# A planner that keeps VectorE's and GpSimd's work on SBUF apart, a memory part one unit later, and weight preparation in pieces

## The chip, the cores and the metric

The kernel runs on one core of a Trainium2 chip. Its time is the device time of one execution in microseconds, as the median of several. The engines are named as in the profile: PE (TensorE, matmuls), DVE (VectorE), ACT (ScalarE), POOL (GpSimd), and SP, whose queue issues the DMAs.

## The reference

Attention with a linear memory beside it, then two feed-forward layers. B, H, S, D = 4, 8, 576, 64; 2304 tokens, width 512, inner widths 2048 and 1536; all in float32.

```python
scores = q @ k.T / sqrt(D), causal mask -1e9
a = exp(scores - max);  a /= a.sum + 1e-9;  local = a @ v
q_p = phi(q)                                  # where(x > 0, x, exp(x) - 1) + 1
mem_out = (q_p @ M_prev) / (q_p @ z_prev + 1e-6)
attn = g * mem_out + (1 - g) * local          # g = sigmoid(beta), by head
h = attn @ w_in;  h = softplus(h) @ w_out
out = ((h @ w_a) * (h @ w_b)) @ w_2
```

## The kernel before

**Attention.** Sixteen units, each a pair of heads of one batch (`Unit`, L428 to L614). Keys and queries are split into a rounded high part and a remainder (`kh`, `kl`, `qh`, `ql`; `prep_k`, made on POOL and ACT, for the first two units on DVE), and a score product is three matmuls: high x high, high x low, low x high (L470, L486). `score(i)` handles rows 128 i to 128 i + 127 of both heads, `score(4)` the 64 rows that are left. DVE reads a score bank, adds the mask, takes the extremum along the row into `mn` and writes the tile `e` (L474, L487; the page calls the instruction CUSTOM_DVE_ANT_0); ACT takes the exponential and sums it into `sm`. `memory` (L494) multiplies `ph`, the phi of the queries, by M and z (L504), takes the reciprocal of the norm in `nm` (L508, L510) and scales the result into `mo` on DVE (L512). `sums` (L517) makes `ss`, the softmax sums, on POOL and scales `mo` by it, also on POOL (L524); `over` makes `rs`, the reciprocals of `ss` (L528, DVE), and spreads them into `R` (L530, POOL). `turn` transposes the exponentials (L541) and copies them scaled by 1 - g into `aT` on ACT (L547) or DVE (L549). `spread` transposes `R` and adds `mo` into the output bank (L585, L589); `use` and `finish` multiply by v (L577, L601, L607) and write `xx`, scaled by `R` (L597, L608).

The loop (L632 to L668) works on two units at once: iteration n scores unit n (`cur`) and finishes unit n-1 (`prev`). `memory` of `cur` stands between `score(1)` and `score(2)`. PE's instructions keep this order. The scores and the memory part take turns on two pairs of PSUM banks, so `score(2)` follows `memory`'s neighbour, and `memory` needs the bank pair that DVE read for `score(0)`, `score(3)` the one from which DVE read `mo`.

**Feed-forward layers.** Each of the layers multiplies by a seven-product scheme over halves of the matrices (`Seven`, L793 and L941). A left part of `w_in`, `w_a` or `w_b` is made by `left_parts`: `decode` turns 64-bit words into float32 in five operations on `raw` (L688, L689 and L691, L693 on DVE, L690 on ACT), then come four sums `wf` (L705), a rounding on ACT and the remainder `w` (L307, DVE). `right_parts` does the like for the inputs, tiles `x1h`, `x1l` and so on. The first three left parts (`FIRST`) and the parts of the first and second third of the attention's output, X[0] and X[1], are made during the attention; the text below calls all of it preparation. The feed-forward matmuls start at the end of the last unit, since they use the same banks.

**The order of the work.** Nothing is issued directly. `Engine` records every operation with its operands as a `Step`; `weigh` (L149) gives it a time, `order` (L198) runs a list schedule over the five engines (on DVE, ACT, POOL and SP the step with the highest rank among those that are ready, on PE the recorded order, attention ahead of the rest), and `emit` issues the result with a wait for every dependence. Each engine then works in that fixed order. Where DVE and POOL both work on SBUF plays no part in `weigh` or `order`.

Of the kernel before, what the change touches and what calls it, by code (L numbers as in the profile page):

```python
# [35 lines left out]
class Step:  # L36


    __slots__ = ("n", "eng", "call", "kw", "line", "deps", "after", "time", "lag", "size", "rank", "stream", "mode", "left", "ready", "start")

# [12 lines left out]
class Plan:  # L53
# [95 lines left out]
    def weigh(self, s):  # L149
# [4 lines left out]
        inp = lambda ap: hasattr(ap, "tensor") and ap.tensor.name == self.psum  # L154
        s.size, s.mode, n = 0, None, size(o)
        if call == "dma_start":
            run = min(self.run(o), self.run(kw["in_"]))
# [3 lines left out]
        elif s.eng == "PE":  # L161
            s.lag = 205
            if call == "transpose":
                s.time = n / 1.2 + 3
                s.mode = 128, 128
            else:
                plain = kw["rhs"].dtype != F32R
                rows, cols = (64 if x <= 64 else 128 for x in (kw["lhsT"].partition_size(), size(kw["lhsT"])))
                s.time = max(2 * (n / 1.2 + 3) if plain else n / 2.4 + 13.3, cols * 0.42 * (128 // rows))
                s.time /= 16384 / rows / cols  # L170
                s.mode = rows, cols
        elif s.eng == "DVE":
            s.lag = 125
            two = call in ("tensor_tensor", "scalar_tensor_tensor", "tensor_tensor_reduce")
            s.time = n / (0.96 if two or any(inp(v) for v in kw.values()) else 1.92) + 68
            if hasattr(kw.get("scalar1"), "tensor"):
                s.time += 64
        elif s.eng == "ACT":
            s.lag = 50 if "accum_out" in kw else 145
            s.time = n * 0.834 + (50 if inp(kw["in_"]) else 94) + (184 if "accum_out" in kw else 0)  # L180
            if not isinstance(kw.get("scale", 1.0), float) or kw.get("scale") == REBIAS:
                s.time += 90
        else:
            s.lag = 90
            s.time = n * 2.1 + 250 if call == "tensor_tensor" else n * 0.9 + 230

# [11 lines left out]
    def order(self):  # L198
# [17 lines left out]
        for s in steps:  # L216
            if not s.left:
                heapq.heappush(soon[s.eng], (0.0, s.n))
        t, lane, done, mode, landed = 0.0, 0.0, 0, None, []
        while done < len(steps):  # L220
            nxt = float("inf")
            moved = False
            for e in engines:
# [10 lines left out]
                if not now[e]:  # L234
                    if soon[e]:
                        nxt = min(nxt, soon[e][0][0])
                    continue
                s = steps[heapq.heappop(now[e])[1]]
                s.start = t
                end = t + s.time  # L240
                if e == "PE":
                    if s.mode != mode:
                        end += SWITCH
                    mode = s.mode
# [43 lines left out]
def tile_kernel(ctx: ExitStack, tc: tile.TileContext, qt, kt, vt, mp, zp, be, w_in, w_out, w_a, w_b, w_2, out):  # L288
# [137 lines left out]
    class Unit:  # L426
# [67 lines left out]
        def memory(self):  # L494
# [6 lines left out]
            for c0, n in ((0, 3), (3, 2)):  # L501
# [7 lines left out]
                pms.append((c0, n, s))  # L509
            V.reciprocal(out=nm, in_=nm)  # L510
            for c0, n, s in pms:
                V.tensor_tensor(  # L512
# [4 lines left out]
        def sums(self):  # L517
# [4 lines left out]
            self.at = []  # L522
            m4 = self.mo.rearrange("p c (j e) -> p c j e", j=2)
            G.tensor_tensor(out=m4, in0=m4, in1=heads(ss, 5), op=ALU.mult)  # L524

# [92 lines left out]
    def attention():  # L618
# [15 lines left out]
        for n in range(nu + 1):  # L634
# [47 lines left out]

    def decode(src, to):

        raw = take("raw").bitcast(U32).rearrange("p (m c) -> p m c", c=2)
        SP.dma_start(out=raw, in_=src)
        low, high = raw[:, :, 0], raw[:, :, 1]
        V.tensor_scalar(out=low, in0=low, scalar1=29, scalar2=None, op0=ALU.logical_shift_right)  # L688
        V.scalar_tensor_tensor(out=low, in0=high, scalar=0x80000000, in1=low, op0=ALU.bitwise_and, op1=ALU.bitwise_or)  # L689
        A.activation(out=f(high), in_=f(high), func=AF.Identity, scale=REBIAS)  # L690
        V.tensor_scalar(out=f(high), in0=f(high), scalar1=MOST, scalar2=-MOST, op0=ALU.min, op1=ALU.max)  # L691
        four = lambda t: t.rearrange("p (b n) -> p b n", b=4)
        V.scalar_tensor_tensor(  # L693
            out=to.bitcast(U32), in0=four(high), scalar=3, in1=four(low), op0=ALU.logical_shift_left, op1=ALU.bitwise_or
        )

    def left_parts(src, at):
# [3 lines left out]
        decode(src, d[:, 0:4])  # L701
# [9 lines left out]
    def right_parts(src, at):  # L711

# [11 lines left out]
        def parts(n, b):  # L724
            rnd(A, x[n][0], b)
            sub(V, x[n][1], b, f(x[n][0]))

# [114 lines left out]

    def left1(u):
        W1[u] = left_parts(w_in[u], at_w[u % 3])

# [12 lines left out]
    for u in FIRST:  # L858
        left1(u)

# [279 lines left out]
```

## Time and profile before

| | |
|---|---|
| median of 3 runs | 1006.91 us (1006.03 to 1007.2) |
| the profiled execution | 1008.35 us, span 1006.6 us |
| PE, DVE, ACT, POOL busy | 962.2, 817.5, 561.9, 115.4 us |
| instructions of PE, DVE, ACT, POOL | 6220, 1312, 1036, 132 |
| PE on the chain that ended last | 76%, DVE 17% |
| POOL's last busy slice | the tenth of 40 slices: the attention |

Busy time counts the instructions that execute, not waits between them; a DVE instruction that is held up by POOL counts as busy while it is held. The granted clock (PEclk) is the share of TensorE's full speed. A unit of attention is taken here as the time from the end of one group of L607 matmuls, the last on PE for a unit, to the end of the next: 33.53, 49.11, 63.45, 78.81, 95.81, 113.53, 125.99, 138.84, 151.57, 164.41, 181.02, 193.47, 205.92, 219.07, 231.66 and 241.91 us.

### The profile page before, as it was taken

The numbers are of one execution on the slowest core, as the hardware profiler recorded it, in microseconds if no ns is written. First come the engines' busy times: TensorE is split into PE (matmuls) and PEld (weight loads), VectorE is DVE, ScalarE is ACT, GpSimd is POOL, SyncE is SP. The second block draws the span as 40 slices with busy tenths as digits, with TensorE's granted clock in tenths as the row PEclk, the third lists the DMA queues.
The fourth block names the chain that finished last, engine by engine and source line by source line (L and its number), as shares of the span: only waits on it lengthen the run. The fifth ranks groups of instructions, "written<-read, shape, count | busy, mean of one in ns | idle before, by whom it ended". The sixth has DMA issues, their size and how long they took to land.

```text
span 1006.6 us, 16653 instructions
## 1 busy us (share of the span) xinstructions
PE 962.2 (96%) x6220; PEld 915.0 (91%) x6220; DVE 817.5 (81%) x1312; ACT 561.9 (56%) x1036; POOL 115.4 (11%) x132
## 2 busy tenths in 40 slices
PE   5987998999999999999999989799999999999998
PEld 4766777778999999999999989799999999999998
DVE  5999899887779853799958997789887665899683
ACT  6776887866666656654545654344443424554453
POOL 4554454441000000000000000000000000000000
PEclk9999899999999999999999999899999999999999
DMA  7342443314888857928273134354663225725611
GB/s 217 106 125 81 115 129 117 105 37 136 267 287 282 290 176 243 330 83 262 84 222 123 67 99 146 114 196 154 221 223 121 104 103 156 253 82 186 205 63 48
DMA packets 76129, 159.96 MB, mean 159 GB/s; under 512 B 11280, under 2 KB 57360, under 8 KB 70928
## 3 DMA queue, kind: packets, MB, share of 16 engines
q1 hardware_dynamic: 75760, 158.57, 47.8%
q8 instruction: 49, 0.80, 0.3%
q10 hardware_dynamic: 288, 0.33, 0.1%
q14 instruction: 32, 0.26, 0.1%
HBM read 104.35 MB, written 54.53 MB: 158 GB/s over the span
## 4 chain that ended last, share of the span: by engine, by line
PE 76%; DVE 17%; issue 2%; DMA 2%; POOL 1%; ACT 1%; DVEq 0%; ACTq 0%; POOLq 0%
PE bank L793 42%; PE bank L941 20%; PE bank L470 3%; PE bank L541 3%; PE bank L577 3%; DVE t L307 2%; PE bank L486 1%; PE bank L589 1%; DVE wf L705 1%; PE bank L504 1%; DVE raw L307 1%; DVE gx2l L307 1%; DVE eFalse L474 1%; DVE gx1l L307 1%; DVE w L307 1%
## 5 line engine op out<-in xcount | busy, mean ns | idle before, releaser
L310 DVE TENSOR_TENSOR s<-bank,s 128x384 f32<-128x384 f32 x216 | 117.2, 553 | 74.5 <-PE bank L793 70.1
L771 ACT ACTIVATE s<-bank 128x384 f32<-128x384 f32 x72 | 34.9, 487 | 88.4 <-PE bank L793 38.3
L793 PE MATMUL bank<-x1h,w 128*128 128x384 f32 x240 | 72.1, 340 | 7.0 <-ACT w L300 3.6
L307 DVE TENSOR_TENSOR t<-t,t 128x1536 f32<-128x1536 f32 (+1 forms) x48 | 74.5, 1555 | 0.8
L793 PE MATMUL bank<-x5h,w 128*128 128x384 f32 x240 | 71.5, 338 | 3.2 <-DVE s L310 3.2
L793 PE MATMUL bank<-x6h,w 128*128 128x384 f32 x240 | 71.2, 337 | 0.0
L793 PE MATMUL bank<-x2h,w 128*128 128x384 f32 x240 | 71.1, 337 | 0.0
L793 PE MATMUL bank<-x4h,w 128*128 128x384 f32 x240 | 71.1, 337 | 0.0
L793 PE MATMUL bank<-x3h,w 128*128 128x384 f32 x240 | 70.5, 334 | 0.0
L793 PE MATMUL bank<-x7h,w 128*128 128x384 f32 x240 | 70.5, 334 | 0.0
L768 ACT ACTIVATE s<-bank 128x384 f32<-128x384 f32 x72 | 34.6, 485 | 42.3 <-PE bank L793 28.3
L690 ACT ACTIVATE raw<-raw 128x1024 f32<-128x1024 f32 x34 | 39.1, 1150 | 29.4 <-DVE raw L689 26.6
L828 ACT ACTIVATE s<-s 128x384 f32<-128x384 f32 x72 | 36.9, 523 | 29.2 <-DVE s L310 29.1
L300 ACT ACTIVATE gx1h<-t 128x768 fp32r<-128x768 f32 x37 | 31.3, 847 | 37.9 <-PE bank L941 32.7
L793 PEld LDWEIGHTS bank<-x1h,w 128*128 128x128 f32 x240 | 44.6, 190 | 8.4 <-DVE w L307 4.3
L300 ACT ACTIVATE gx2h<-t 128x768 fp32r<-128x768 f32 x37 | 31.3, 846 | 34.8 <-PE bank L941 29.7
L300 ACT ACTIVATE gx0h<-t 128x768 fp32r<-128x768 f32 x37 | 31.3, 846 | 31.9 <-PE bank L941 23.6
L478 ACT ACTIVATE eTrue<-eTrue,mn 128x384 f32<-128x384 f32 (+1 forms) x64 | 42.2, 661 | 11.8 <-DVE mn L474 11.8
L793 PEld LDWEIGHTS bank<-x5h,w 128*128 128x128 f32 x240 | 44.7, 190 | 3.6 <-DVE s L310 3.5
L774 ACT ACTIVATE s<-bank 128x384 f32<-128x384 f32 x72 | 35.2, 489 | 22.0 <-PE bank L793 16.3
L470 PE MATMUL bank<-kh,qh 64*128 64x128 f32 (+3 forms) x128 | 31.8, 425 | 15.2 <-DVE kh L302 9.7
L300 ACT ACTIVATE w<-wf 128x1792 fp32r<-128x1792 f32 x20 | 34.1, 1704 | 21.3 <-DVE wf L705 21.0
(329 smaller groups left out, 3132.8 us busy)
## 6 DMA issues: line engine op xcount, KB each, us to landing
gs<-s SPq DMA_DIRECT2D x96, 192.0 KB, 4.1
t<-gs SPq DMA_DIRECT2D x24, 768.0 KB, 4.9
us<-s SPq DMA_DIRECT2D x72, 192.0 KB, 3.1
t<-us SPq DMA_DIRECT2D x12, 768.0 KB, 4.7
raw<-w_in SPq DMA_DIRECT2D x8, 1024.0 KB, 6.1
raw<-w_out SPq DMA_DIRECT2D x8, 1024.0 KB, 7.0
raw<-w_a SPq DMA_DIRECT2D x6, 1024.0 KB, 5.6
raw<-w_b SPq DMA_DIRECT2D x6, 1024.0 KB, 5.7
```

Of the source, the lines that this page charges most:

```text
L300: A.activation(out=o, in_=i, func=AF.Copy)
L307: eng.tensor_tensor(out=o, in0=a, in1=b, op=ALU.subtract)
L310: eng.tensor_tensor(out=o, in0=a, in1=b, op=ALU.add)
L470: PE.matmul(out=s[:, j, :L], lhsT=a[r, qc], rhs=b[r, 0:L], start=t == 0, stop=t == 2)
L478: A.activation(out=e, in_=e, func=AF.Exp, scale=-1.0, bias=mn[:, n : n + 1], accum_out=sm[:, n : n + 1])
L690: A.activation(out=f(high), in_=f(high), func=AF.Identity, scale=REBIAS)
L768: A.activation(out=self.s1, in_=bank["b"], func=AF.Copy)
L771: A.activation(out=self.s5, in_=bank["c"], func=AF.Copy)
L774: A.activation(out=self.s2, in_=bank["b"], func=AF.Copy)
L793: PE.matmul(out=o, lhsT=w(n, a, k), rhs=x[n][c][:, k], start=start and k == t == 0, stop=k == 1 and t == 2, skip_group_check=True,)
L828: A.activation(out=s, in_=s if bank is None else bank, func=AF.Softplus)
L941: PE.matmul(out=o, lhsT=self.w[n][a][:, u, 128 * m : 128 * m + 128], rhs=x[c][:, j], start=start and u == t == 0, stop=u == self.nu - 1 an ...
```

## The change

`weigh` marks steps that use SBUF in a way that can meet the other engine's: every POOL step, and a DVE step of more than 64 columns that neither reads nor writes PSUM. While such a step of one engine runs in the plan, `order` starts none of the other: it takes another ready step, or lets the engine stand. A marked POOL step also gets a real dependence on the last marked DVE step before it; a DVE step gets none on POOL. `memory` is called for `prev` instead of `cur`, behind the first two `turn`s, and once more after the last unit; the factor `ss` is multiplied into `nm` (128x10, DVE) in place of POOL's instruction on `mo` (128x640). `decode` of the first three left parts works in two halves, their rounding and remainder in four pieces of two, two, two and one seventh; the parts of X[0] are rounded and subtracted in two halves.

```diff
@@ weigh
+        two = call in ("tensor_tensor", "scalar_tensor_tensor", "tensor_tensor_reduce")
+        s.port = s.eng == "POOL" or s.eng == "DVE" and not any(inp(v) for v in kw.values()) and n > 64
@@ order
-        t, lane, done, mode, landed = 0.0, 0.0, 0, None, []
+        t, lane, done, mode, landed, held = 0.0, 0.0, 0, None, [], {"DVE": 0.0, "POOL": 0.0}
+        port = None
...
-                s = steps[heapq.heappop(now[e])[1]]
+                s = steps[now[e][0][1]]
+                if s.port and held[e] > t:
+                    free_ = [x for x in now[e] if not steps[x[1]].port]
+                    if not free_:
+                        nxt = min(nxt, held[e])
+                        continue
+                    s = steps[min(free_)[1]]
+                now[e].remove(next(x for x in now[e] if x[1] == s.n))
+                heapq.heapify(now[e])
                 s.start = t
                 end = t + s.time
+                if s.port:
+                    held["POOL" if e == "DVE" else "DVE"] = end
+                    if e == "DVE":
+                        port = s.n
+                    elif port is not None:
+                        s.deps.add(port)
@@ Unit.memory, Unit.sums
             V.reciprocal(out=nm, in_=nm)
+            V.tensor_tensor(out=nm, in0=nm, in1=self.ss, op=ALU.mult)
...
-            m4 = self.mo.rearrange("p c (j e) -> p c j e", j=2)
-            G.tensor_tensor(out=m4, in0=m4, in1=heads(ss, 5), op=ALU.mult)
@@ attention
+            if cur:
+                cur.prep_v2()
             if prev:
                 prev.turn(A, [(0, 0)])
                 prev.turn(V, [(1, 0)])
-            if cur:
-                cur.prep_v2()
-                cur.memory()
-            if prev:
+                prev.memory()
                 prev.turn(A, [(0, 1), (0, 3)])
@@ decode
-    def decode(src, to):
+    def decode(src, to, step=4):
...
+        for b in range(0, 4, step):
+            low, high = (four(raw[:, :, i])[:, b : b + step] for i in range(2))
...
@@ left_parts
-        rnd(A, w[:, :, 0], d)
-        sub(V, w[:, :, 1], d, f(w[:, :, 0]))
+        for n in range(0, 7, step):
+            e = min(n + step, 7)
+            rnd(A, w[:, n:e, 0], d[:, n:e])
+            sub(V, w[:, n:e, 1], d[:, n:e], f(w[:, n:e, 0]))
@@ right_parts
-            rnd(A, x[n][0], b)
-            sub(V, x[n][1], b, f(x[n][0]))
+            for k in range(0, 2, step):
+                u = slice(k, k + step)
+                rnd(A, x[n][0][:, u], b[:, u])
+                sub(V, x[n][1][:, u], b[:, u], f(x[n][0][:, u]))
@@ feed-forward, before the first unit
     for u in FIRST:
-        left1(u)
+        left1(u, 2)
+    X[0] = right_parts(xs[0], X_AT[0], 1)
```

The order of DVE's instructions where one unit passes into the next, before, in the unit that ends at 95.81 us: `ph`, preparation (`wf`), `xx` of the unit that ends, then the first score reads (ISA) of the next.

```order
L457 SCALAR_TENSOR_TENSOR ph_77<-ph_77,pos_78 128x640
L705 TENSOR_TENSOR wf<-wf 128x256 x3
L528 RECIPROCAL rs_129<-ss_127 128x10
L705 TENSOR_TENSOR wf<-wf 128x256 x3
L597 TENSOR_TENSOR xx_118<-bank,rb_117 128x512
L608 TENSOR_TENSOR xx_118<-bank,rb_117 128x64
L705 TENSOR_TENSOR wf<-wf 128x256
L474 ISA eFalse_87,mn_122<-bank,mask_56 128x128
```

The same place after, two units later in the program (L473 is L457 of before, L720 L705, L323 L307, L490 L474):

```order
L473 SCALAR_TENSOR_TENSOR ph_76<-ph_76,pos_78 128x640
L323 TENSOR_TENSOR w<-wf,w 128x2x256
L323 TENSOR_TENSOR w<-wf,w 128x256
L720 TENSOR_TENSOR wf<-wf 128x256 x3
L612 TENSOR_TENSOR xx_118<-bank,rb_117 128x512
L543 RECIPROCAL rs_129<-ss_127 128x10
L623 TENSOR_TENSOR xx_118<-bank,rb_117 128x64
L490 ISA eFalse_87,mn_122<-bank,mask_56 128x128
```

The preparation stands between `ph` and `xx`, in pieces; none is left between `xx` and the score reads.

DVE behind the first score reads of a unit, before: the whole remainder `w` of a left part, then the memory part of the current unit.

```order
L307 TENSOR_TENSOR w<-wf,w 128x7x256
L508 TENSOR_SCALAR nm_125<-bank 128x6
L508 TENSOR_SCALAR nm_125<-bank 128x4
L510 RECIPROCAL nm_125<-nm_125 128x10
L512 TENSOR_TENSOR mo_101<-bank,nm_125 128x384
L512 TENSOR_TENSOR mo_101<-bank,nm_125 128x256
```

After, the same place, with the memory part of the unit before:

```order
L323 TENSOR_TENSOR w<-wf,w 128x2x256
L564 TENSOR_SCALAR aT_106<-bank,og_60 128x512
L524 TENSOR_SCALAR nm_125<-bank 128x6
L720 TENSOR_TENSOR wf<-wf 128x256
L524 TENSOR_SCALAR nm_125<-bank 128x4
L526 RECIPROCAL nm_125<-nm_125 128x10
L527 TENSOR_TENSOR nm_125<-nm_125,ss_127 128x10
L529 TENSOR_TENSOR mo_101<-bank,nm_125 128x384
L529 TENSOR_TENSOR mo_101<-bank,nm_125 128x256
```

A remainder of two sevenths and one `wf` stand there, and L527 is the new multiplication.

POOL's order in one unit, before:

```order
L304 TENSOR_SCALAR kh_73<-kr_65 128x576
L307 TENSOR_TENSOR kl_75<-kr_65,kh_73 128x576
L521 TENSOR_SCALAR ss_127<-sm_121 128x9
L521 TENSOR_SCALAR ss_127<-sm_121 128x1
L524 TENSOR_TENSOR mo_101<-mo_101,ss_127 128x640
L530 TENSOR_SCALAR R_104<-rs_129 128x512
L307 TENSOR_TENSOR ql_71<-qr_67,qh_69 128x640
```

And after:

```order
L320 TENSOR_SCALAR kh_72<-kr_64 128x576
L323 TENSOR_TENSOR kl_74<-kr_64,kh_72 128x576
L538 TENSOR_SCALAR ss_126<-sm_120 128x9
L538 TENSOR_SCALAR ss_126<-sm_120 128x1
L323 TENSOR_TENSOR ql_70<-qr_66,qh_68 128x640
L545 TENSOR_SCALAR R_104<-rs_128 128x512
```

`mo` is gone, and `ql` stands ahead of `R`.

## Rows read from the trace of the kernel before

**Rows 1.** The page, busy time by engine.
```profile
PE 962.2 (96%) x6220; PEld 915.0 (91%) x6220; DVE 817.5 (81%) x1312; ACT 561.9 (56%) x1036; POOL 115.4 (11%) x132
```
**Rows 2.** Windows: length, busy time by engine (count), granted clock, DMA share, GB/s.
```profile
33.53:231.66 198.13, 181.67 (x1695) 144.26 (x1696) 180.87 (x476) 149.45 (x392) 95.71 (x96) 0.96 0.32 97
...
241.91:1006.60 764.69, 749.07 (x4273) 746.01 (x4273) 605.72 (x762) 385.31 (x581) 0.00 (x0) 0.99 0.52 173
```
**Rows 3.** Windows, four single units (PE, PEld, DVE, ACT, POOL).
```profile
63.45:78.81 15.36, 12.91 (x124) 9.88 (x123) 15.10 (x36) 10.71 (x28) 9.59 (x9) 1.00 0.28 80
95.81:113.53 17.72, 14.95 (x123) 12.01 (x123) 16.55 (x37) 12.04 (x29) 6.70 (x7) 0.81 0.23 69
164.41:181.02 16.61, 13.67 (x124) 11.33 (x123) 15.27 (x36) 10.42 (x28) 7.08 (x8) 0.90 0.38 122
181.02:193.47 12.45, 12.41 (x123) 9.83 (x123) 9.31 (x31) 9.68 (x27) 6.77 (x9) 1.00 0.26 76
```
**Rows 4.** Waits of PE, 33.53 to 231.66: total us, times, longest.
```profile
PE bank L504 <- DVE mn L474: 10.3, 5, 2.9
PE bank L470 <- DVE mo L512: 5.1, 6, 1.9
```
**Rows 5.** Timeline of PE: start, us, instruction, in brackets the wait before it.
```profile
66.70 1.38 PE L504 MATMUL bank<-mz,ph 128*128 128x130 f32 x10 [1.34 <-DVE mn L474]
...
169.26 2.53 PE L504 MATMUL bank<-mz,ph 128*128 128x130 f32 x10 [2.94 <-DVE mn L474]
```
**Rows 6.** Timeline of all engines, 74 to 80, the SBUF instructions of DVE and POOL.
```profile
74.46 1.40 POOL L307 TENSOR_TENSOR kl<-kr,kh 128x576 fp32r<-128x576 f32 x1
...
75.17 1.37 DVE L457 SCALAR_TENSOR_TENSOR ph<-ph,pos 128x640 f32<-128x640 f32 x1
...
75.94 1.78 POOL L521 TENSOR_SCALAR ss<-sm 128x9 f32<-128x9 f32 x2
...
77.81 1.26 POOL L524 TENSOR_TENSOR mo<-mo,ss 128x640 f32<-128x640 f32 x1
...
77.89 4.34 DVE L705 TENSOR_TENSOR wf<-wf 128x256 f32<-128x256 f32 x4
...
79.04 0.79 POOL L530 TENSOR_SCALAR R<-rs 128x512 f32<-128x512 f32 x1
```
**Rows 7.** Timeline of DVE, 12.5 to 14.1, where POOL does nothing.
```profile
12.53 0.82 DVE L307 TENSOR_TENSOR ql<-qr,qh 128x640 fp32r<-128x640 f32 x1
13.26 0.82 DVE L457 SCALAR_TENSOR_TENSOR ph<-ph,pos 128x640 f32<-128x640 f32 x1
```
**Rows 8.** Lines by form, DVE, from 242 on (no POOL): busy us, mean ns | idle before.
```profile
L705 DVE TENSOR_TENSOR wf<-wf 128x256 f32<-128x256 f32 x68 | 28.8, 423 | 1.6
...
L307 DVE TENSOR_TENSOR raw<-raw,raw 128x768 f32<-128x768 f32 x12 | 11.3, 953 | 0.1
```
**Rows 9.** Lines by form, DVE, 33.53 to 231.66.
```profile
L457 DVE SCALAR_TENSOR_TENSOR ph<-ph,pos 128x640 f32<-128x640 f32 x13 | 16.1, 1236 | 0.0
...
L705 DVE TENSOR_TENSOR wf<-wf 128x256 f32<-128x256 f32 x12 | 10.0, 836 | 0.2
...
L307 DVE TENSOR_TENSOR raw<-raw,raw 128x768 f32<-128x768 f32 x5 | 8.1, 1625 | 0.0
...
L307 DVE TENSOR_TENSOR x2l<-raw,x2h 128x768 fp32r<-128x768 f32 x2 | 2.9, 1442 | 0.0
...
L307 DVE TENSOR_TENSOR x7l<-raw,x7h 128x768 fp32r<-128x768 f32 x1 | 2.0, 1992 | 0.0
```
**Rows 10.** Lines by form, POOL, 33 to 232.
```profile
L524 POOL TENSOR_TENSOR mo<-mo,ss 128x640 f32<-128x640 f32 x15 | 20.2, 1347 | 1.3
L307 POOL TENSOR_TENSOR kl<-kr,kh 128x576 fp32r<-128x576 f32 x12 | 17.0, 1413 | 1.0
...
L304 POOL TENSOR_SCALAR kh<-kr 128x576 fp32r<-128x576 f32 x12 | 8.1, 674 | 76.0 <-PE bank L486 76.0
```
**Rows 11.** Timeline of PE, the first unit's memory part.
```profile
12.65 2.54 PE L504 MATMUL bank<-mz,ph 128*128 128x130 f32 x10 [0.85 <-POOL mz L419]
```

More of the change, by code (lines that the diff above doesn't have):

```diff
@@ L36 @@
 class Step:
-    __slots__ = ("n", "eng", "call", "kw", "line", "deps", "after", "time", "lag", "size", "rank", "stream", "mode", "left", "ready", "start")
+    __slots__ = ("n", "eng", "call", "kw", "line", "deps", "after", "time", "lag", "size", "rank", "stream", "mode", "port", "left", "ready", "start")
 class Engine:
@@ L173, in weigh @@
             s.lag = 125
-            two = call in ("tensor_tensor", "scalar_tensor_tensor", "tensor_tensor_reduce")
             s.time = n / (0.96 if two or any(inp(v) for v in kw.values()) else 1.92) + 68
@@ L184, in weigh @@
             s.lag = 90
-            s.time = n * 2.1 + 250 if call == "tensor_tensor" else n * 0.9 + 230
+            s.time = n * 2.1 + 250 if two else n * 0.9 + 230
     @staticmethod
@@ L681, in tile_kernel, with left_parts @@
     PASSES = ((0, 0), (0, 1), (1, 0))
-    def decode(src, to):
+    def decode(src, to, step=4):
         raw = take("raw").bitcast(U32).rearrange("p (m c) -> p m c", c=2)
         SP.dma_start(out=raw, in_=src)
[L687 to L691, printed above, removed]
-        four = lambda t: t.rearrange("p (b n) -> p b n", b=4)
[L693 to L697, printed above, removed]
+        four = lambda t: t.rearrange("p (b n) -> p b n", b=4)
+        for b in range(0, 4, step):
+            low, high = (four(raw[:, :, i])[:, b : b + step] for i in range(2))
+            V.tensor_scalar(out=low, in0=low, scalar1=29, scalar2=None, op0=ALU.logical_shift_right)
+            V.scalar_tensor_tensor(out=low, in0=high, scalar=0x80000000, in1=low, op0=ALU.bitwise_and, op1=ALU.bitwise_or)
+            A.activation(out=f(high), in_=f(high), func=AF.Identity, scale=REBIAS)
+            V.tensor_scalar(out=f(high), in0=f(high), scalar1=MOST, scalar2=-MOST, op0=ALU.min, op1=ALU.max)
+            V.scalar_tensor_tensor(
+                out=to.bitcast(U32)[:, b : b + step], in0=high, scalar=3, in1=low, op0=ALU.logical_shift_left, op1=ALU.bitwise_or
+            )
+    def left_parts(src, at, step=7):
         w, d = (t.rearrange("p (n h m) -> p n h m", n=7, h=2) for t in twice("w", 3584, at))
         d = d[:, :, 1]
-        decode(src, d[:, 0:4])
+        decode(src, d[:, 0:4], min(step, 4))
         a21, a22, a11, a12 = (d[:, n] for n in range(4))
@@ L705, in left_parts, with right_parts @@
             V.tensor_tensor(out=o, in0=a, in1=b, op=op)
-        rnd(A, w[:, :, 0], d)
-        sub(V, w[:, :, 1], d, f(w[:, :, 0]))
+        for n in range(0, 7, step):
+            e = min(n + step, 7)
+            rnd(A, w[:, n:e, 0], d[:, n:e])
+            sub(V, w[:, n:e, 1], d[:, n:e], f(w[:, n:e, 0]))
         slot = {5: 0, 4: 1, 1: 2, 2: 3, 7: 4, 6: 5, 3: 6}
         return lambda n, h, k: w[:, slot[n], h, 128 * k : 128 * k + 128]
-    def right_parts(src, at):
+    def right_parts(src, at, step=2):
         x = {
@@ L841, in spill_out, with left1 @@
             SP.dma_start(out=wod[:, :, u], in_=t)
-    def left1(u):
-        W1[u] = left_parts(w_in[u], at_w[u % 3])
+    def left1(u, step=7):
+        W1[u] = left_parts(w_in[u], at_w[u % 3], step)
     def made1(i, u, g):
```

## The prediction

> **What bounds the kernel now.** I read the page first, then busy time by stretch, then the attention unit by unit. PE is busy 96% of the span and DVE 81% [rows 1], but these are means over two stages. The span falls into a start of 33.53 us (the first unit), fourteen more units of attention in 198.13 us, a last one of 10.25 us, and 764.69 us in which PE is busy 749 [rows 2]. What the change rewrites lies in the first 242 us; behind that the engines' instructions keep their order almost word for word, so I look for the result in the 198.13 us.
>
> A unit has a floor there. The one from 181.02 takes 12.45 us with PE busy 12.41 at full clock; DVE needs 9.31 and has no weight preparation in it. The unit from 63.45 takes 15.36 with DVE busy 15.10, and the one from 95.81 17.72 with DVE 16.55 and PE at a granted clock of 0.81, in which it is busy 14.95 for the same work [rows 3]. So DVE, loaded with preparation, makes a unit long. The waits say the same: PE waits 10.3 us at L504 for `mn`, that is, until DVE has read the first scores and their bank is free, and 5.1 us at L470 for `mo` [rows 4]. Behind a wait of 2.94 us L504 x10 takes 2.53, behind one of 1.34 it takes 1.38 [rows 5]: a long wait also costs clock. Fourteen units at 12.45 would be 174.3 us, so 23.8 us is all that can be had here.
>
> Part of DVE's load is waiting for POOL where both work on SBUF. At 75.17 `ph` takes 1.37 us, and POOL's `kl` runs until 75.86; at 77.89 four small subtractions `wf` take 4.34 us while POOL runs `mo` and `R` [rows 6] and then `ql`. Alone, `ph` takes 0.82 [rows 7], a `wf` 0.423 and `raw` 128x768 0.953 [rows 8]; the `x` differences have the same 768 columns. In the fourteen units they take 1.236 (x13), 0.836 (x12), 1.625 (x5), and two `x` groups 1.442 (x2) and 1.992 [rows 9]. The excess: 13 x 0.42 = 5.4, 12 x 0.41 = 5.0, 5 x 0.67 = 3.4, 2 x 0.49 + 1.04 = 2.0: 15.8 us of DVE's 180.87 [rows 2]. Smaller groups are left uncounted.
>
> **The change, part by part.** *POOL's `mo` goes.* That is 15 x 1.35 = 20.2 us of POOL in this stretch [rows 10], and the instruction that ran into the preparation. In its place DVE multiplies 128x10, which the trace does not show. From 256 columns at 0.423 and 768 at 0.953 [rows 8] a column costs 1.04 ns and an instruction 0.16 us besides; that is my price, bounds 0.1 and 0.25: 14 x 0.16 = 2.2 us more on DVE.
>
> *Pieces.* DVE gets 21 instructions more for the three weights and 7 for the `x` parts. By the same 0.16, of which I take half since the next one starts before the last has ended (`ph` starts 0.09 before the end of `ql` in [rows 7]): 28 x 0.08 = 2.2 us; bounds 0 and 4.5. ACT gets 19 pieces more; at a full 0.16 and twice that it is at most 6 us beside its 149.45 of 198.13 [rows 2], which PE's work covers.
>
> *The new order.* Before, preparation stands in clumps: none in the unit from 181.02, seven `wf` and a `w` of 1792 columns in others, the `w` ahead of `nm` and `mo`, for which PE waits. After, each unit from the second to the twelfth has three to five pieces behind `ph` and one or two small ones by `nm`. The sum over the fourteen units stays nearly the same: what the slack units lacked is moved into them. This is what shortens the path, since a unit at the floor has 12.45 - 9.31 = 3.1 us of DVE to give.
>
> *The port.* POOL's `kh`, `ql` and most of `R` now stand beside score and copy instructions that read PSUM; the slowed groups of [rows 9] are all SBUF to SBUF. But `kl` is made to wait for `ph`, and right behind `ph` come the pieces. Only POOL gets a wait: in the plan DVE stands idle during `kl`, on the chip it starts its first piece, `kl` follows, and the second piece stands behind `kl`. Price: 1.41 [rows 10] less 0.1 for the start, 1.3 us, in the eleven units with at least two pieces there: 14.3 us. Bounds: 0, if POOL never gets in between, and 11 x 1.41 = 15.5. I take the upper side, since at 77.8 us `mo`, `wf`, `R`, `wf` take turns: four `wf` need 1.7 alone and took 2.6 more, of which `mo` and `R` hold 1.26 and 0.79 [rows 6], and `ql` the rest.
>
> By the Trainium skill (Perfetto Trace Analysis, GPSIMD Engine Instruction) a POOL span in a profile is unreliable, and the spacing of starts is the better measure. From `kl` at 74.46 to `ss` at 75.94 the spacing is 1.48 us against a span of 1.40 [rows 6]; the trace bears it out a little, and by the spacing the eleven units would cost 0.9 us more.
>
> *Waits added.* `kh`, `kl`, `ss`, `ql` and `R` each wait for DVE's last SBUF instruction. Behind them on POOL stands the `ql` of the next unit, needed almost a unit later; POOL waits 76.0 us for PE at `kh` [rows 10], which is its slack, some 5 us a unit: no cost until it is used up. `ss` now comes behind the pieces; DVE's `rs`, which needs it, has `xx` and mostly the score reads in front: nothing, or 0.3 a unit if `ss` is slow. `memory` moves from the current to the previous unit at the same place of PE's stream; its `mo` is due only at the end of that iteration. The weight loads on SP keep their order against each other.
>
> *Start and end.* The first unit loses its L504, 2.54 us behind a wait of 0.85 [rows 11]; but the second unit's `kh`, `kl`, `ql` (0.82 for `ql` [rows 7]) move behind all five score reads, and PE then waits for them, some 2 us; the last unit gains an L504 of about 1.3 [rows 5]. 3.4 - 2.0 - 1.3: nothing, bounds -2 and +2.5.
>
> **The sum.** DVE in the fourteen units: 180.9 - 15.8 + 14.3 + 2.2 + 2.2 = 183.8 us, 13.1 a unit, above PE's 12.45. A DVE-bound unit leaves DVE idle 15.36 - 15.10 = 0.26 [rows 3], 14 x 0.26 = 3.6: 187.4 against 198.1. The last two of the fourteen have no `kl`, and shares of lighter units carry over: about 1 us less. Gain 12. The profiled execution took 1008.35 us, 1.75 around its span; the median of the runs is 1006.91, from which I subtract: 995.
>
> **Rivals.**
> *A: the port wait really goes.* The pieces hide `kl`, or POOL loses each race. For it: behind `ph` PE has some 3 us of products that need DVE for nothing. Against: the turns in [rows 6]. DVE 183.8 - 14.3 = 169.5 is below PE's floor; 174.3 and 0.2 a unit make 177, a gain of 21: 986.
> *B: more collisions than `kl`.* `R` (0.79 at 79.04 [rows 6]) runs into the small pieces by `nm`, and these and the new multiplication hold up `mo`, for which L470 waits already [rows 4]. 11 x 0.5 takes 5.5 of the gain: 1000.5. By the Trainium skill (SBUF — State Buffer, Who interferes with whom) issue order decides which of the two blocks, for the whole instruction; by that rule every POOL instruction that starts first is paid by DVE, which has no wait on POOL here.
> *C: no change.* What the spreading gains is lost again, in POOL's waits or behind 242 us: 1006.
> *D: slower.* The pieces and `kl` overrun the gap behind `ph`, DVE reads the first scores late, and PE waits at L504 in each of the eleven units. Where that wait grows to some 2 us, between the 1.34 and 2.94 of [rows 5], the clock falls, and units take 16.61 as the one from 164.41 [rows 3]. Eleven at 16.6 and three at 12.5 are 220: +22, 1029. Against: a load of 13.1 us leaves a mean wait of 0.7.
>
> **How the numbers follow.** Forecast 0.50, A 0.22, B 0.18, C 0.05, D 0.05. The forecast's own range: `kl`, pieces and multiplication at their dear ends +4.8, or the cheap ends -3.0 without `kl`, start and end 2 either way: 990 to 1002. With most of A and all of B inside: 985 to 1002, which leaves out C, D and some of A. A measurement tells a change from none at about 0.2%, 2 us: faster 0.91, same 0.04, slower 0.05.
>
> **What would show it.** Right: no `mo` on POOL; `wf` and `raw` at their time alone but for one piece a unit, behind `kl`, some 1.3 us over; units of 12.5 to 13.6 us at full clock; L504 waits under 1 us; 765 us behind the attention. Wrong: units at 12.45 without a slowed piece (A); slowed pieces by `nm` and waits for `mo` (B); units of 16 us at a clock of 0.8 to 0.9 (D).

## Result and profile after: 989.8 us against 1006.5, ratio 0.9835 [0.9818, 0.9852]

The changed kernel takes 989.82 us (median of four runs, 988.82 to 991.19), the kernel before beside it 1006.47. The time lies between the forecast (995) and rival A (986), just outside the forecast's own range of 990 to 1002 and inside the whole one of 985 to 1002. The profiled execution took 990.1 us, span 988.0.

The page, busy time by engine, answers to [rows 1]: DVE has 44 instructions more and 8.3 us less, POOL 16 fewer and 39 us less.
```profile
PE 953.6 (97%) x6220; PEld 908.9 (92%) x6220; DVE 809.2 (82%) x1356; ACT 564.1 (57%) x1055; POOL 76.3 (8%) x116
```
Busy time by stretch, cut at the ends of units as in [rows 2] (length, then PE, PEld, DVE, ACT, POOL, granted clock, DMA share, GB/s):
```profile
0.00:32.97 32.97, 21.13 (x153) 17.20 (x153) 21.77 (x62) 22.62 (x57) 13.99 (x33) 0.90 0.65 203
32.97:213.36 180.39, 173.82 (x1695) 137.81 (x1696) 172.98 (x518) 151.18 (x409) 62.29 (x83) 1.00 0.35 107
213.36:223.54 10.18, 10.08 (x101) 8.46 (x100) 8.27 (x17) 4.88 (x9) 0.00 (x0) 1.00 0.44 161
223.54:988.00 764.46, 748.55 (x4276) 745.43 (x4276) 606.21 (x762) 385.46 (x581) 0.00 (x0) 0.99 0.52 173
```
The spans of the two profiled executions differ by 18.6 us (1006.6 and 988.0), the medians by 16.65. Of the 18.6 us, 17.74 lie in the fourteen units (198.13 to 180.39), 0.56 in the start; the last unit and the 764 us behind it gave 0.3. The 17.74 split in two. PE's busy time fell by 7.85 us for the same 1695 matmul groups; 6.8 of it fell in the four units that stood at a granted clock of 0.81 to 0.90 before and at 1.00 after. PE's idle time fell from 198.13 - 181.67 = 16.46 to 180.39 - 173.82 = 6.57.

Two units, beside [rows 3]: where before ran from 12.45 to 17.72 us at clocks down to 0.81, after stays between 12.44 and 13.30 at full clock.
```profile
84.60:97.58 12.98, 12.50 (x124) 9.84 (x123) 12.64 (x39) 11.35 (x31) 4.46 (x5) 1.00 0.33 95
174.90:187.34 12.44, 12.29 (x123) 9.86 (x123) 10.94 (x36) 11.22 (x30) 5.71 (x8) 1.00 0.36 112
```
Waits of PE in the fourteen units, beside [rows 4]. The 10.3 us of the memory part's matmuls (now L520) behind the first score reads are gone; what is left is `score(3)` behind `mo`, no longer in six waits of up to 1.9 us but in thirteen of up to 0.8.
```profile
PE bank L486 <- DVE mo L529: 6.4, 13, 0.8
```
DVE's lines by form in the fourteen units, beside [rows 9] (busy us, mean ns | idle before). `wf` and the 768-column `raw` stand at or near their time alone [rows 8], 0.418 and 0.965 against 0.423 and 0.953; `ph` is still slowed, 1.21 against 0.82 [rows 7]. The new L527 took 0.17 us in twelve of the units and 0.63 and 0.57 in two, in which POOL worked on `mz`, the tile of M and z.
```profile
L473 DVE SCALAR_TENSOR_TENSOR ph<-ph,pos 128x640 f32<-128x640 f32 x13 | 15.7, 1208 | 0.0
...
L720 DVE TENSOR_TENSOR wf<-wf 128x256 f32<-128x256 f32 x12 | 5.0, 418 | 0.2
...
L323 DVE TENSOR_TENSOR raw<-raw,raw 128x768 f32<-128x768 f32 x5 | 4.8, 965 | 0.0
...
L527 DVE TENSOR_TENSOR nm<-nm,ss 128x10 f32<-128x10 f32 x14 | 3.3, 232 | 0.5
```
The timeline of DVE and POOL in the unit that ends at 97.58, the place of [rows 6] (start, us, instruction, wait before it). `kl` starts right behind POOL's own `kh`, ahead of `ph`, and it is `ph` that is held: 1.39 us. The pieces behind it run alone, three `wf` in 1.33 where [rows 6] had four in 4.34; POOL's `ss` waits for the last of them, and `ql` runs beside score reads.
```profile
92.48 0.68 POOL L320 TENSOR_SCALAR kh<-kr 128x576 fp32r<-128x576 f32 x1 [4.67 <-PE bank L502]
...
93.25 1.41 POOL L323 TENSOR_TENSOR kl<-kr,kh 128x576 fp32r<-128x576 f32 x1
93.36 0.68 DVE L576 TENSOR_TENSOR aT<-bank,og 128x512 f32<-128x512 f32 x1
93.95 1.39 DVE L473 SCALAR_TENSOR_TENSOR ph<-ph,pos 128x640 f32<-128x640 f32 x1
95.27 0.68 DVE L323 TENSOR_TENSOR w<-wf,w 128x512 fp32r<-128x512 f32 x1
95.87 1.33 DVE L720 TENSOR_TENSOR wf<-wf 128x256 f32<-128x256 f32 x3
...
97.89 0.48 POOL L538 TENSOR_SCALAR ss<-sm 128x9 f32<-128x9 f32 x2 [3.23 <-DVE w L323]
...
98.45 1.56 POOL L323 TENSOR_TENSOR ql<-qr,qh 128x640 fp32r<-128x640 f32 x1
```
The same timeline 5 us later, the memory part: a piece `w` of 0.77 us stands between the two halves of `nm`, then come the reciprocal, the new L527 and `mo`; PE stands 0.54 us for `mo`.
```profile
100.36 0.77 DVE L323 TENSOR_TENSOR w<-wf,w 128x512 fp32r<-128x512 f32 x1
...
101.24 0.22 DVE L526 RECIPROCAL nm<-nm 128x10 f32<-128x10 f32 x1
...
101.49 0.17 DVE L527 TENSOR_TENSOR nm<-nm,ss 128x10 f32<-128x10 f32 x1
101.69 0.89 DVE L529 TENSOR_TENSOR mo<-bank,nm 128x384 f32<-128x384 f32 x2
102.30 0.83 PE L486 MATMUL bank<-kh,qh 64*128 64x512 f32 x2 [0.54 <-DVE mo L529]
```

### The profile page after: what moved, and what is told of

It is laid out like the page before. It is cut to its first block, busy times and chain, and to the rows that moved or that the text cites. A ratio compares the mean times of both kernels' runs of the same rounds, so it can differ in the third digit from the quotient of the medians.

```text
span 988.0 us, 16697 instructions
## 1 busy us (share of the span) xinstructions
PE 953.6 (97%) x6220; PEld 908.9 (92%) x6220; DVE 809.2 (82%) x1356; ACT 564.1 (57%) x1055; POOL 76.3 (8%) x116
## 4 chain that ended last, share of the span: by engine, by line
PE 73%; DVE 22%; issue 2%; ACT 1%; DMA 1%; POOL 0%; DVEq 0%; POOLq 0%
PE bank L812 43%; PE bank L961 20%; PE bank L486 3%; DVE t L323 2%; PE bank L556 2%; PE bank L592 2%; DVE aT L564 1%; DVE eFalse L490 1%; DVE gx1l L323 1%; DVE gx2l L323 1%; DVE raw L323 1%; DVE w L323 1%; DVE mo L529 1%; DVE wf L720 1%; DVE gx3l L323 1%
## 5 line engine op out<-in xcount | busy, mean ns | idle before, releaser
L323 DVE TENSOR_TENSOR t<-t,t 128x1536 f32<-128x1536 f32 (+1 forms) x48 | 74.5, 1554 | 0.8
L706 ACT ACTIVATE raw<-raw 128x1024 f32<-128x1024 f32 (+1 forms) x37 | 39.4, 1073 | 19.1 <-DVE raw L705 16.2
L812 PEld LDWEIGHTS bank<-x4h,w 128*128 128x128 f32 x240 | 44.9, 191 | 0.0
```

What stands on the lines that cost most here:

```text
L323: eng.tensor_tensor(out=o, in0=a, in1=b, op=ALU.subtract)
L812: PE.matmul(out=o, lhsT=w(n, a, k), rhs=x[n][c][:, k], start=start and k == t == 0, stop=k == 1 and t == 2, skip_group_check=True,)
```

## Experiments

### Which of the three parts gains

The change has three parts: the **rule** (`s.port` and `held` in `weigh` and `order`), the **memory** part (one unit later, `ss` multiplied into `nm`), and the **pieces** (`left1(u, 2)`, `right_parts(.., 1)`). Each was put alone into the kernel before, and each was taken alone out of the kernel after.

The rule alone, on the kernel before:
```diff
@@ weigh
+        s.port = s.eng == "POOL" or s.eng == "DVE" and not any(inp(v) for v in kw.values()) and n > 64
@@ order
+                if s.port and held[e] > t:
...
+                    held["POOL" if e == "DVE" else "DVE"] = end
...
+                    elif port is not None:
+                        s.deps.add(port)
```


> The kernel before with the planner's rule on SBUF alone. Theory 1 (the order carries the gain): 994 to 1000, more than half of the 16.7 us. Theory 3 (POOL's instruction on mo was the whole trouble): 1004 to 1007.

The memory part alone, on the kernel before:
```diff
@@ Unit.memory, Unit.sums, attention
+            V.tensor_tensor(out=nm, in0=nm, in1=self.ss, op=ALU.mult)
...
-            G.tensor_tensor(out=m4, in0=m4, in1=heads(ss, 5), op=ALU.mult)
...
-                cur.memory()
...
+                prev.memory()
```


> The kernel before with the memory part one unit later and ss multiplied into nm on DVE, nothing else. Theory 1: the 20.2 us of mo leave POOL, and with them the collisions of mo with wf, raw and x, some 0.8 us in eight units, 6 us; the clumps of preparation stay: 999 to 1002. Theory 3: 990 to 993.

The pieces alone, on the kernel before:
```diff
-        left1(u)
+        left1(u, 2)
+    X[0] = right_parts(xs[0], X_AT[0], 1)
```


> The kernel before with the pieces alone. Theory 1: collisions stay and there are more instructions to collide; the 2.0 us w no longer stands whole in front of nm, which gives back a wait for mo of 1.9 us at most three times: 1002 to 1008. Theory 2 (pieces give the gain): 992 to 997.

After without the pieces:
```diff
-        left1(u, 2)
-    X[0] = right_parts(xs[0], X_AT[0], 1)
+        left1(u)
```


> The changed kernel with the left parts and X[0] made whole, as before: the planner's rule on SBUF and the later memory part stay. Theory 1 (the gain of 16.7 us is DVE time that POOL's instructions no longer hold, and preparation spread evenly; both come from the order): most of the gain stays, 992 to 995; a whole w of 2.0 us in front of nm costs PE a wait for mo of about 1.5 us in the three units that have one. Theory 2 (the pieces give the gain, since a short instruction blocks nothing): 1000 to 1004.

After without the rule:
```diff
@@ order
-                if s.port and held[e] > t:
...
-                    elif port is not None:
-                        s.deps.add(port)
```


> The changed kernel without the planner's rule on SBUF (no stretch in which DVE or POOL is kept off, no wait of POOL on DVE); later memory part and pieces stay. Theory 1: preparation goes back into the early units and beside ql and R; DVE's instructions are held again by about 0.6 us for each R and 1.3 for each ql that meets one: 996 to 1000. Theory 2 (pieces) or theory 3 (POOL's mo was the whole trouble): 989 to 992, nearly nothing lost.

After without the memory part:
```diff
-            V.tensor_tensor(out=nm, in0=nm, in1=self.ss, op=ALU.mult)
...
+            G.tensor_tensor(out=m4, in0=m4, in1=heads(ss, 5), op=ALU.mult)
...
-                prev.memory()
...
+                cur.memory()
```


> The changed kernel with the memory part in the current unit and mo scaled on POOL, as before; rule and pieces stay. Theory 1: mo holds POOL 1.35 us more per unit, and the plan has to keep DVE's pieces off it or let them meet: 1.3 us in some eleven units, less what the plan hides beside PSUM work, 993 to 999. Theory 3: without this part nothing is left of the gain, 1003 to 1007.

Medians, ratio to the kernel before timed beside it, and the fourteen units of the profiled execution:

| rule | memory | pieces | us | ratio [95%] | units |
|---|---|---|---|---|---|
| x | | | 984.34 | 0.9772 [0.9750, 0.9794] | 175.87 |
| | x | | 1005.65 | 0.9987 [0.9973, 1.0002] | 195.22 |
| | | x | 1016.87 | 1.0098 [1.0075, 1.0121] | 208.07 |
| x | x | | 996.65 | 0.9889 [0.9855, 0.9923] | 186.18 |
| | x | x | 1012.34 | 1.0053 [1.0033, 1.0072] | 203.02 |
| x | | x | 983.73 | 0.9767 [0.9738, 0.9795] | 174.97 |
| x | x | x | 989.82 | 0.9835 [0.9818, 0.9852] | 180.39 |

The gain is the rule's: alone it gives 22 us, more than the whole change. The memory part costs 6 us in the full change and 12 without the pieces, and without the rule it gives nothing alone and 5 us beside the pieces. The pieces alone lose 11 us, win 7 beside rule and memory part, and do nothing beside the rule alone.

The fourteen units with the rule alone, and PE's waits in them: idle time of PE falls to 175.87 - 174.12 = 1.75 us, the clock is full, DVE is busy 167.49 us instead of 180.87 with two instructions more, and the preparation is whole, not in pieces.
```profile
32.65:208.52 175.87, 174.12 (x1699) 138.22 (x1699) 167.49 (x478) 149.59 (x391) 82.63 (x99) 1.00 0.35 110
```
```profile
PE bank L486 <- DVE mo L528: 1.2, 3, 0.7
```
The rule does two things at once. It keeps DVE's and POOL's instructions apart, and it spreads the preparation: DVE is busy between 10.98 and 12.55 us in a unit, where before it was between 9.31 and 16.76. In the three units of before that DVE loaded most (16.76, 16.55 and 15.27 us), 1.2 to 2.6 us each are time held by POOL, an estimate from what each instruction took at its shortest in these traces; some 14 us would be left, more than the 12.45 of a unit at the floor. So by this estimate both are needed, but no run does one without the other, and none takes apart the planner's order and POOL's real wait on DVE.

The pieces alone: the fourteen units, one unit, and PE's waits. More instructions meet POOL, the score reads come later, the memory part's matmuls (L506 here) wait up to 3.4 us for them, and the unit shown takes 18.07 us at a clock of 0.81. This is rival D's chain, in a kernel without the rule.
```profile
32.59:240.66 208.07, 184.29 (x1696) 146.24 (x1696) 190.94 (x502) 153.58 (x411) 93.08 (x96) 0.94 0.30 93
60.96:79.03 18.07, 14.66 (x124) 11.96 (x123) 16.82 (x41) 11.14 (x29) 7.75 (x8) 0.81 0.22 68
```
```profile
PE bank L506 <- DVE mn L476: 17.4, 8, 3.4
```
Without the pieces, after has its waits for `mo` in longer stretches, and two of its units fall to a clock of 0.89, at 15.28 and 15.50 us.
```profile
PE bank L486 <- DVE mo L529: 8.7, 12, 1.6
```
```profile
86.87:102.37 15.50, 13.92 (x124) 11.43 (x123) 14.42 (x36) 12.05 (x29) 4.68 (x6) 0.89 0.26 79
```

### What `kl` costs beside `ph`, and behind it

After, with `ph` recorded ahead of `prep_k`, and `kl` made to wait for it and free to run beside DVE: the order that the prediction had priced.
```diff
-            if nxt and n:
-                nxt.prep_k()
             if cur:
                 cur.prep_v2()
+                behind = len(plan.steps) - 1
+            if nxt and n:
+                nxt.prep_k()
+                plan.steps[-2].deps.add(behind)
+                plan.steps[-2].port = False
```


> The changed kernel with the order that the prediction had read into it: POOL's kl waits for ph, and the pieces follow ph without regard to kl. The prediction's price is 1.3 us for the piece behind kl in eleven units, in place of the 0.4 to 0.6 by which ph is held now: 13 x 0.39 = 5 us back and 14.3 more, 995 to 1000. If pieces and kl take turns without DVE losing more than it does now: 988 to 991.

Measured 1004.15 us, 0.9967 [0.9952, 0.9982]: 14.3 us over after. `kl` now waits for `ph` and runs into the second instruction behind it; `raw`, 0.56 us nine us earlier, takes 1.65. DVE and POOL in the second of the fourteen units, then the window of all of them:
```profile
57.89 0.81 DVE L473 SCALAR_TENSOR_TENSOR ph<-ph,pos 128x640 f32<-128x640 f32 x1
58.62 0.68 DVE L708 SCALAR_TENSOR_TENSOR raw<-raw 128x512 uint32<-128x512 uint32 x1
58.85 1.74 POOL L323 TENSOR_TENSOR kl<-kr,kh 128x576 fp32r<-128x576 f32 x1 [1.75 <-DVE ph L473]
59.23 1.65 DVE L710 TENSOR_SCALAR raw<-raw 128x512 f32<-128x512 f32 x1
```
```profile
32.72:224.35 191.63, 177.88 (x1695) 138.12 (x1696) 182.77 (x519) 152.34 (x411) 67.22 (x83) 1.00 0.33 103
```
DVE's 182.77 us are 9.8 more than after's 172.98; by the prediction's price it would be 14.3 less the 5.0 that `ph` no longer loses, 9.3. So its price for DVE was right; its order wasn't the kernel's. The time is another matter: 995 to 1000 had been expected, and 1004 is outside. The fourteen units grew by 11.2 us, since PE also waits longer for `mo` (9.8 us in place of 6.4) and again for `mn` at L520 (2.6), and its products took 4.1 us more at the same granted clock. That the medians differ by the same 14.3 as the price is chance.

After, with `kl` recorded and ordered behind `ql`, so that it meets neither `ph` nor the pieces:
```diff
-            sub(e, self.kl, kr, f(self.kh))
...
+            sub(e, self.kl, kr, f(self.kh))
+            if not first:
+                plan.steps[-1].deps.add(len(plan.steps) - 2)
```


> The changed kernel with POOL's kl recorded and ordered behind ql of the same unit, so that it no longer meets ph; it then stands beside score reads and copies from PSUM. In the changed kernel ph takes 1.21 in the mean against 0.82 alone, 13 x 0.39 = 5.1 us, and DVE idles 0.26 a unit. If DVE bounds the units, most of that comes back: 985 to 987. If PE's wait for mo (6.4 us in 13 waits) bounds them, nothing: 989 to 990.

998.56 us, 0.9927 [0.9903, 0.9951]: slower than after, though `ph` took 0.829 instead of 1.208, and outside both expectations. The collision was not gone, it had moved. `kl` now runs beside `nm`, and the multiplication of `nm` by `ss` (L527 in after, L529 here), 10 columns that the rule leaves unmarked since they are not more than 64, is held until `kl` ends. It took 1.12 to 1.13 us in six units and 0.82 in one, against 0.17 alone; the reciprocal just before it, with one input, took its 0.22 beside the same `kl`.
```profile
91.21 1.41 POOL L323 TENSOR_TENSOR kl<-kr,kh 128x576 fp32r<-128x576 f32 x1
91.28 0.22 DVE L528 RECIPROCAL nm<-nm 128x10 f32<-128x10 f32 x1
91.53 1.12 DVE L529 TENSOR_TENSOR nm<-nm,ss 128x10 f32<-128x10 f32 x1
92.68 0.89 DVE L531 TENSOR_TENSOR mo<-bank,nm 128x384 f32<-128x384 f32 x2
93.30 1.12 PE L488 MATMUL bank<-kh,qh 64*128 64x512 f32 x2 [1.52 <-DVE mo L531]
```
```profile
PE bank L488 <- DVE mo L531: 9.9, 9, 1.5
```
These seven units are the ones that took 13.28 us or more, four of them at a clock of 0.89; the other seven took 12.42 to 13.02. The fourteen together are 191.08 us. So this run doesn't show what the collision at `ph` costs after. It shows that even a very small instruction pays the whole rest of a POOL instruction, and that `mo` bounds the unit.

### Why the memory part costs time

In after, a plan without a look ahead starts a piece when DVE is free for a moment, and `nm` and `mo` stand behind it. Two experiments go at one suspect each. First the pieces by `nm`: `order` starts no preparation on DVE if an attention instruction becomes ready within six tenths of its length.
```diff
@@ order
+                near = [r for r, x in soon[e] if e == "DVE" and s.stream and not steps[x].stream and r < t + 0.6 * s.time]
+                if near:
+                    nxt = min(nxt, min(near))
+                    continue
                 if s.port and held[e] > t:
```


> The changed kernel, but the plan starts no preparation instruction on DVE if an attention instruction becomes ready on DVE within six tenths of its length; this takes nearly all pieces away from in front of `nm` and `mo`. Theory 1 (a piece in front of `nm` and `mo` makes PE wait for `mo` before `score(3)`): these waits fall from 6.4 us to under 2, time 984 to 986. Theory 2 (the memory part one unit later costs by its new multiplication L527, 0.17 to 0.23 us in the chain from `nm` to `mo`, whatever stands in front): waits of 0.2 to 0.3 us in every unit stay, 3 to 4 us, time 987 to 988. Theory 3 (the loss is not at `mo`): 989 to 991.

Then L527: the memory part still one unit later, pieces where they were, but `ss` multiplied into `mo` by POOL, behind DVE's `mo`.
```diff
-            V.tensor_tensor(out=nm, in0=nm, in1=self.ss, op=ALU.mult)
...
+            G.tensor_tensor(out=m4, in0=m4, in1=heads(self.ss, 5), op=ALU.mult)
```


> The changed kernel with the memory part still one unit later, but its factor `ss` put on `mo` by POOL's instruction again, behind DVE's `mo`; the multiplication L527 is gone, one piece of preparation still stands in front of `nm` and `mo` in most units. Theory 1 (the piece is the cost): waits of PE for `mo` stay at 4 to 6 us, time 987 to 990. Theory 2 (L527 is the cost): waits fall below 3 us, time 984 to 987. If POOL's `mo` ran into DVE's preparation: above 990, with preparation instructions at twice their time.

985.90 us, 0.9796 [0.9780, 0.9813], and 986.69 us, 0.9801 [0.9787, 0.9814]. PE's waits for `mo`, first with the look ahead, then with POOL's multiplication:
```profile
PE bank L490 <- DVE mo L533: 1.8, 6, 0.5
```
```profile
PE bank L486 <- DVE mo L528: 2.8, 7, 0.6
```
Both theories got the time and wait they had named for their own suspect, so neither holds alone. The fourteen units are 176.27 us in each, 4.1 less than in after. The look ahead did not take nearly all pieces away, as had been expected: in eight of the fourteen units one still stands between `nm` and `mo`, as in after, but it delays `mo` by at most some 0.2 us more. A look at the second kernel's unit that answers to the one above shows L527's share: the same piece stands between the halves of `nm`, `mo` follows 0.25 us behind the reciprocal instead of 0.45, and PE waits 0.31 us instead of 0.54.
```profile
98.37 0.77 DVE L323 TENSOR_TENSOR w<-wf,w 128x512 fp32r<-128x512 f32 x1
...
99.25 0.22 DVE L526 RECIPROCAL nm<-nm 128x10 f32<-128x10 f32 x1
...
99.50 0.89 DVE L528 TENSOR_TENSOR mo<-bank,nm 128x384 f32<-128x384 f32 x2
...
100.11 0.83 PE L486 MATMUL bank<-kh,qh 64*128 64x512 f32 x2 [0.31 <-DVE mo L528]
```
The piece and L527 are links of one chain, from PE's L520 over `nm` to `mo`. From the end of PE's L520 to the start of `mo` the timelines of after show 1.02 us in the mean of the fourteen units (0.70 to 1.36), those with the look ahead 0.76, those with POOL's multiplication 0.75, and those of the fastest kernel below, which has neither piece nor L527 there, 0.48 or 0.49 in every unit. PE has other products for about 0.55 us of it: where `mo` starts 1.09 us behind L520, PE waits 0.54, and where it starts after 0.48, not at all. Either experiment takes more than half of the listed wait (6.4 us to 1.8, or to 2.8).

Where the memory part stays with the current unit, no piece stands between `nm` and `mo` in any of the fourteen units. In that kernel's trace POOL's `mo`, `R` and `ql` stand beside the score reads and `nm`, and by the rule DVE's pieces have to go elsewhere. That this is why the place stays free wasn't tested by itself; the two kernels with `kl` behind `ql` speak for it, in which POOL's `kl` stands beside `nm` and one piece and none are left there. Another 1.0 us of the memory part's cost is the last unit, which gains an L520: 10.18 us in after, 9.18 without.

### Two more versions

The look ahead and `kl` behind `ql` together, on after:
```diff
+                near = [r for r, x in soon[e] if e == "DVE" and s.stream and not steps[x].stream and r < t + 0.6 * s.time]
...
+                plan.steps[-1].deps.add(len(plan.steps) - 2)
```


> The changed kernel with the same look ahead, and POOL's `kl` recorded behind `ql`, so that it stands beside the score reads instead of `ph`. Theory 1: `ph` falls from 1.21 to 0.83 us (13 x 0.38 = 5 us of DVE), waits for `mo` stay under 2 us, time 982 to 985. Rival: the collision with `kl` is hidden behind PE's products that need nothing of DVE, then the time is that of the kernel with the look ahead alone, within 1.5 us.

987.61 us (983.75 to 987.98), 0.9801 [0.9782, 0.9820], not better than the look ahead alone: 1.7 us above its median, where the rival had allowed 1.5, with overlapping intervals. `ph` fell to 0.816 and DVE's busy time in the fourteen units from 167.35 to 162.73, yet these units are only 0.75 us shorter, and the last one and what follows lost it again. So the rival had the time nearly right, but its reason, that the collision at `ph` lies beside products that need nothing of DVE, is only half shown. With the look ahead alone, `ph` is held in four units, and these take 12.72 to 12.85 us; the nine with a free `ph` take 12.43 to 12.66. Without the hold some 0.3 us in each of four units is won; but `kl` now held the multiplication of `nm` in three units (0.77, 0.52 and 0.23 us), and the first two of them took 13.03 and 12.79. Where the memory part stays with the current unit, the hold is hidden: in the fastest kernel below, six units with `ph` held take 12.22 to 12.43 us, and six with `ph` free 12.22 to 12.46.
```profile
L479 DVE SCALAR_TENSOR_TENSOR ph<-ph,pos 128x640 f32<-128x640 f32 x13 | 10.6, 816 | 0.0
```
```profile
32.98:208.50 175.52, 172.52 (x1696) 137.89 (x1696) 162.73 (x504) 149.00 (x404) 61.74 (x81) 1.00 0.35 111
```

Rule, pieces and look ahead, with the memory part of before:
```diff
@@ after without the memory part, order
+                near = [r for r, x in soon[e] if e == "DVE" and s.stream and not steps[x].stream and r < t + 0.6 * s.time]
+                if near:
+                    nxt = min(nxt, min(near))
+                    continue
```


> The kernel with the planner's rule and the pieces but the memory part as it was before, with the look ahead. Without it this kernel took 983.7 us with units at 12.45 us, PE's floor, and 0.5 us of waits for `mo`. Theory 1: nothing is left to win by the look ahead in the fourteen units, 982 to 985. Rival: preparation kept out of the attention runs late into the last unit, 986 to 990.

980.43 us (979.57 to 983.64), 0.9752 [0.9735, 0.9769]: the lowest median of all, below what either theory expected, though its interval overlaps those of the rule alone and of rule and pieces. Against after, the intervals are apart. Its fourteen units, and behind them:
```profile
32.61:206.19 173.58, 173.38 (x1699) 138.22 (x1699) 163.73 (x493) 149.32 (x404) 78.36 (x96) 1.00 0.36 111
...
215.37:977.60 762.23, 746.33 (x4273) 743.22 (x4272) 609.52 (x769) 385.82 (x583) 0.00 (x0) 0.99 0.52 175
```
PE is idle for 0.2 us in fourteen units by busy time: the order of DVE and POOL has next to nothing more to give there. Against the same kernel without the look ahead the spans differ by 4.6 us (982.2 and 977.6); only 1.4 of it lie in the fourteen units, 3.4 lie behind the attention, and what gave those was not looked into.

## Why the prediction was right, and which term was mis-sized

- **What bounds, and where the gain lies:** right. 17.74 of 18.6 us fell in the fourteen units; start, last unit and the end were set at nothing and gave 0.56, 0.07 and 0.23.
- **Collisions of the preparation:** right in kind and in size. `wf` and `raw` are near their time alone. Of the groups that I had summed to 15.8 us, `ph` keeps 13 x (1.208 - 0.82) = 5.0 us and the others next to nothing.
- **The failed term is `kl`, 14.3 us.** The step that failed is "`kl` is made to wait for `ph`". Nothing makes it: on POOL it starts right behind `kh`, and `kh` had waited for PE, not for DVE. In the plan `kl` stands ahead of `ph`; on the chip DVE arrives early, finds `kl` running and loses 0.57 us at `ph` itself in the unit shown, not 1.3 at a piece behind it. I had read from the orders of both engines which instruction follows which on each, and had taken an order between the engines from it; the waits of `kl`, not its neighbours, tell that. What `kl` costs DVE is the 5.0 us at `ph`. The experiment with `kl` behind `ph` shows that the price would have held for the order that I had assumed: DVE 182.77 us against 172.98 in after.
- **Moving the memory part "at the same place of PE's stream", at no cost:** wrong by 6 us, the second term that failed. I had followed when `mo` is used, not when its banks are read out: `score(3)` needs the bank from which DVE reads `mo`, whoever's `mo` it is, and the move put a piece and L527 in front of it.
- **Luck in the number:** the two errors pull in opposite directions. With 5.0 in place of 14.3 the sum gives DVE 183.8 - 9.3 = 174.5 us, 12.46 a unit, at PE's floor: rival A's 986. The measured 990 lies between that and the forecast because the memory part, set at nothing, took 6 us back.
- **Multiplication and pieces:** L527 took 0.232 in the mean, price 0.16, so 3.3 us for 2.2; by itself it took 0.17, and the rest are the two units in which POOL's `mz` held it. DVE by the mended sum: 180.9 - 15.8 + 5.0 + 3.3 + 2.2 = 175.6; measured 172.98. The rest of 2.6 would mostly be the smaller groups that were left uncounted: with the rule alone the three groups of `raw` with 1024 columns fell by 2.7 us. The pieces cost DVE 169.18 - 167.49 = 1.7 us beside the rule, price 2.2.
- **"A DVE-bound unit":** wrong with the term for `kl`. DVE is idle 180.39 - 172.98 = 7.4 us. Units end by PE's work and its wait for `mo`: of PE's 6.57 idle us, 6.4 are that wait.
- **Rival A** was right that the pieces behind `ph` run free, but `ph` itself still pays, and units are not at the floor, except the one of 12.44 us. **Rival B's** mechanism was there in part: the small pieces by `nm` hold up `mo`. It was priced at 5.5 us, and the look ahead gave 3.9 (989.82 to 985.90); but `R` beside them wasn't needed for it, and the new L527 holds a like share.
- **The new order:** that preparation is spread over the units is right, and the rule alone does it. The pieces aren't needed for it: with the rule alone, whole groups lie as well in the units (175.87) as pieces do (174.97). The pieces help only beside the moved memory part, which leaves the place by `nm` open.
- **The clock:** the forecast's sum has no term for it; only rival D names it. The four units of before at 0.81 to 0.90 are gone with their waits, and with them 6.8 of the 17.74 us.

## What to carry to other kernels

Before pricing a collision of two engines, read which instruction waits for which across them; neighbours in two separate orders don't say who comes first. An instruction that sets when a bank comes free is on the path even if its result is due much later, and a planner without a look ahead will put filler in front of it. A rule that keeps engines apart must not leave small instructions out: the one of 10 columns, left unmarked, stood on the path and was held for 0.95 us. When a change has several parts, time each alone and each left out: here one part gave more than the whole, and another took a quarter of it back.

## What the runs showed of the hardware

What POOL held in these runs were above all DVE's instructions with two inputs from SBUF; one that reads PSUM wasn't held. Beside the same `kl`, `aT` from a bank took its 0.68 us and `ph` 1.39 instead of 0.82. `kl` started 0.70 us before `ph` and ended 0.71 us after `ph` started, and `ph` lost 0.57: about the whole rest of `kl`, not a share of it. In the kernel with `kl` behind `ql` the multiplication of 128x10 took 1.12 instead of 0.17 and ended 0.03 us behind `kl`, while the reciprocal of 128x10 just before it, with one input, wasn't held. The Trainium skill (SBUF — State Buffer, Who interferes with whom) says that a DVE instruction with two SBUF inputs contends with a POOL instruction that reads SBUF, and one with at most one SBUF input, outside the two-port modes, doesn't; `ph`, the multiplication, the reciprocal and `aT` agree with it. `raw` with its one input was held as well (1.65 us in the experiment with `kl` behind `ph`), which by that page would take a two-port mode; no run here shows in which mode it ran.

PE's floor for a unit was not the 12.45 us that I had read. In the fastest kernel four units took 12.22 or 12.23 us and nine took 12.42 to 12.46, all at full clock and with no idle time of PE to speak of. Two neighbours:
```profile
57.27:69.50 12.23, 12.23 (x123) 9.85 (x123) 11.85 (x36) 10.58 (x29) 7.09 (x11) 1.00 0.53 177
69.50:81.95 12.45, 12.42 (x123) 9.83 (x123) 11.69 (x37) 10.45 (x29) 5.66 (x7) 1.00 0.32 101
```
The 0.2 us stand in front of the transposition of `R` (L605). Its first weight load (PEld) starts 0.11 us behind the load before it in the short units and 0.35 to 0.40 behind in the long ones, and in each of the nine long ones 0.11 to 0.12 us after ACT has copied `aT` out of a bank (L567), one of the set from which `R` takes its own. So in the long units PE waits there for ACT, a wait that the view gives as "issue" and that PE's busy time hides.
```profile
63.81 0.84 ACT L567 ACTIVATE aT<-bank,og 128x256 f32<-128x256 f32 x2 [0.23 <-PE bank L561]
64.78 0.47 PEld L605 LDWEIGHTS bank<-ident,R 128*128 128x128 f32 x4
...
76.35 0.81 ACT L567 ACTIVATE aT<-bank,og 128x256 f32<-128x256 f32 x2
77.28 0.42 PEld L605 LDWEIGHTS bank<-ident,R 128*128 128x128 f32 x4 [0.24 <-issue]
```
